# Key sums by fp32 adds on VectorE, one tile transposed by DMA, two denominators side by side: a linear-attention and MLP block on one core

## The chip, the core and the metric

The kernel runs on one core of one Trainium2 chip. The metric is the device time of one execution in microseconds, as the median of several runs. A core has TensorE (matmuls into PSUM, whose eight banks hold 128 x 512 fp32 each), VectorE, ScalarE and GpSimd, which work on SBUF and, GpSimd apart, on PSUM, and SyncE, whose queue here issues every DMA. Each engine takes its instructions in the order of its own queue. In the views of the profile PE is TensorE, PEld its weight loads, DVE VectorE, ACT ScalarE, POOL GpSimd and SP (SPq) SyncE.

## What is computed

```python
def phi(t): return where(t > 0, t + 1, exp(t)) + 1e-6

# A: linear attention, S = 2048 tokens, D = 512, 32 heads of 16
q, k, v = split(layernorm(x) @ wqkv)        # per head
pq, pk  = phi(q), phi(k)
kv  = einsum("bhsd,bhse->bhde", pk, v)
z   = einsum("bhsd->bhd", pk)               # sum of the keys over all tokens
num = einsum("bhqd,bhde->bhqe", pq, kv)
den = einsum("bhqd,bhd->bhq", pq, z)[..., None] + 1e-6
h   = x + merge_heads(num / den) @ wo
# B: MLP with 512 -> 1792 -> 512
out = h + relu(layernorm(h) @ w1) @ w2
```

Inputs and output are bf16.

## The kernel before

The 2048 tokens are 16 tiles of 128 tokens and 4 blocks (chunks, numbered 0 to 3) of 512 tokens. Everything stays in SBUF. There are no loops over tiles in the program: the string ORDER lists about 700 words, each the name of a small operation with its arguments, and they are issued in that order. The order in which the words stand is the order of each engine's queue. Semaphores between the engines follow from the data, and each PSUM bank is named by hand in the words.

The words that matter here, with their lines in the kernel before:

- `lx.t.n` (L219) loads n token tiles from tile t, `lk`, `lq`, `lv`, `lo`, `l1`, `l2` (L222) load parts of the key, query, value, output, first and second MLP weights. `lq.0.2` and `lq.2.2` are the two halves of the query weights along the contraction.
- `S.t`, `A.t` (L237, L238): layernorm statistics of tile t and their aggregate, on VectorE. `R` (L243, L244): 1/std on ScalarE. `N.t` (L251): the normalised tile. `s`, `a`, `r`, `n` are the same for the second layernorm (L239, L240, L243, L244, L258).
- A normalised tile is transposed into `lnT` either on TensorE, `T.t` (L270, four 128 x 128 transposes into PSUM, then a copy `E.t` on ScalarE, L280, or `V.t` on VectorE, L283), or by a DMA, `X.t` (L291). For the second layernorm: `t.t` with `e.t` or `v.t` (L270, L286, L289), or `x.t` (L292).
- `K.t` (L299): the keys of tile t, four matmuls of 128 x 512. `Q.c.j` (L307): a quarter j of the transposed queries of block c.
- phi of keys: `F` (L317, Exp) and `U` (L320, Relu) on ScalarE, `M` (L324, min with 1, plus 1e-6) and `D` (L327, add) on VectorE, for two tiles in one instruction in most places. `qF`, `qU`, `qM`, `qD` are the same for queries, L317 to L327.
- `G.t` (L351): four matmuls that add tile t's share to the product of the normalised tokens and the keys, in PSUM banks 4 to 7, over all 16 tiles. `gA`, `gD` (L373, L376) copy it out.
- `z.j` (L359): quarter j of the sum of the keys over the tokens, by 16 matmuls, one for each tile, each with a 128 x 128 weight load of keys and one column of ones. `zc`, `zh` (L365, L368) copy it and spread it over heads.
- `kv`, `kx`, `m` (L381, L389, L393), `mD` (L399): the small products that give, for each head, one matrix m that holds kv and wo.
- Denominators: `d4.c` (L406, four matmuls for block c), `dl4`, `dx4` (L412, L417: Ln, then Exp of minus that, on ScalarE, into `ld` and `rd`). For block 0 they are spread to rows by `rp` and `rm` on TensorE and VectorE (L422, L428), for blocks 1 to 3 they go through DRAM: `wb.c` (L434), eight `rb.c.h` (L437), and `dm` (L444) multiplies the queries by them.
- `h.t`, `hD.t` (L453, L459): the attention output and its addition to x.
- `p.c.f` and `ph` (L468, and L477 for half blocks): the MLP's up-projection; `pA`, `pD` (L483, L488): Relu on ScalarE or VectorE. `f.t` (L497): the down-projection of a tile, `fo` (L505) the scaled addition, `fd` (L512) the store.
- `warm` (L234): matmuls on zeros at the start.

The keys of tiles 0 and 1 lie in `pk_lo`, those of tiles 2 to 15 in a buffer that the MLP uses later (`acts[0]`). In the order before, tiles 0 to 5 are transposed on TensorE and 6 to 15 by DMA; for the second layernorm, tiles 0 to 3 on TensorE and the others by DMA.

Of the kernel before, what the change touches and what calls it, by code (L numbers as in the profile page):

```python
# [15 lines left out]


ORDER = """
table const masks warm.70.7.64 warm.3.7 lx.0.1 S.0 lx.3.1 lx.2.1 lx.1.1 S.3 S.2 A.0 A.3 A.2 R.0.1 S.1 R.2.2
N.0.2.2 A.1 N.0.0.2 N.2 R.1.1 N.3 N.1 lk.0.2 lx.4.2 lk.2.2 T.0.3.2.2 warm.1.7 T.0.0.0.2 T.2.2 E.0.2.2 T.3.3  # L20
T.1.1 V.2 E.0.0.2 E.1 K.0.0 lx.6.2 S.4 E.3 S.5 A.5 A.4 F.0.1 R.4.2 U.0.1 S.7 S.6 M.0.1 N.4 K.2.2 K.1.1 F.1.1
U.1.1 K.3.3 D.0.1 A.6 A.7 R.6.2 M.1.1 N.5 lx.8.4 D.1.1 N.7 T.4.0 G.0 T.5.1 F.2.1 E.4 E.5 U.2.1 S.9 S.8 N.6
M.2.1 A.9 A.8 D.2.1 F.3.1 R.8.2 U.3.1 G.1 K.4.0 K.5.1 F.4.2 U.4.2 M.3.1 S.10 N.8 D.3.1 A.10 S.11 M.4.2 N.9
D.4.2 A.11 lx.12.4 lq.2.2 X.7 X.6 lv.0.2 R.10.2 G.2 K.7.3 G.3 K.6.2 F.6.2 U.6.2 lq.0.2 X.8 X.9 S.13 S.12 A.13
N.11 N.10 A.12 M.6.2 X.11 X.10 D.6.2 R.12.2 G.4 G.5 K.8.0 K.9.1 F.8.2 U.8.2 N.13 S.14 N.12 S.15 A.14 A.15
M.8.2 D.8.2 R.14.2 N.15 N.14 G.6 G.7 K.11.3 K.10.2 X.13 X.12 lo.2.2 X.14 X.15 l1.2.2 l2.0.7 lo.0.2 l1.0.2
lv.2.2 l2.7.7 F.10.2 U.10.2 G.8 G.9 K.12.0 K.13.1 U.12.2 F.12.2 M.10.2 D.10.2 M.12.2 G.10 K.14.2 K.15.3
Q.0.0.0 Q.0.1.1 G.11 F.14.2 U.14.2 M.14.2 D.12.2 G.12 D.14.2 qF.0.0.2 qU.0.0.2 G.13 z.1.2 G.14 Q.0.3.1 z.0.2
Q.0.2.0 G.15 z.2.2 z.3.2 qU.0.2.2 qF.0.2.2 gD.0.2 zc gA.2.2 qM.0.0.2 Q.1.1.3 Q.1.0.2 qF.1.0.2 qU.1.0.2 kv.1.4
kv.0.4 kv.3.4 kv.2.4 zh qM.0.2.2 qD.0.0.2 qD.0.2.2 kx Q.1.2.0 m.0.4 m.1.5 d4.0.3 m.3.7 m.2.6 Q.1.3.1 dl4.0  # L30
dx4.0 Q.2.1.3 qF.1.2.2 qU.1.2.2 qM.1.0.2 mD.0.2 mD.2.2 rp.0.0.4 rp.0.3.7 rp.0.1.5 rp.0.2.6 Q.2.0.2 qM.1.2.2
rm.0.0.2 rm.0.2.2 qD.1.0.2 qD.1.2.2 Q.2.3.1 Q.2.2.0 qU.2.0.2 qF.2.0.2 h.0.4 h.1.5 Q.3.0.2 Q.3.1.3 hD.0 hD.1
s.0 s.1 a.0 h.2.6 a.1 n.0 n.1 hD.2 qF.2.2.2 qU.2.2.2 h.3.7 t.0.4 qU.3.0.2 qF.3.0.2 e.0 Q.3.2.0 d4.1.4 t.1.5
Q.3.3.1 hD.3 s.2 s.3 a.2 a.3 n.2 n.3 v.1 t.2.6 dl4.1 dx4.1 qF.3.2.2 qU.3.2.2 v.2 t.3.7 wb.1 ph.0.1.3.0
ph.0.0.2.0 rb.1.0 rb.1.4 rb.1.2 rb.1.6 rb.1.1 rb.1.7 rb.1.5 rb.1.3 v.3 ph.0.1.3.1 ph.0.0.2.1 pD.0.0.2 qM.2.2.2
ph.0.3.1.1 ph.0.2.0.0 ph.0.2.0.1 ph.0.3.1.0 p.0.4.2 p.0.5.3 pA.0.2.2 p.0.6.0 p.0.7.1 pA.0.6.2 pD.0.4.2 p.0.8.2
p.0.9.3 p.0.11.1 p.0.10.0 pA.0.8.2 dm.1.0.2 dm.1.2.2 h.6.6 hD.6 h.5.5 p.0.13.3 h.7.7 hD.5 qM.3.0.2 s.6 a.6 s.5
qM.2.0.2 n.6 a.5 qD.2.2.2 h.4.4 hD.4 f.2.6.0.7 p.0.12.2 s.4 qD.2.0.2 qD.3.0.2 qM.3.2.2 hD.7 a.4 n.5 s.7 a.7
pA.0.10.2 pA.0.12.2 r.0.4 n.7 n.4 f.0.4.0.7 f.0.4.7.7 f.2.6.7.7 f.3.7.0.7 fo.0 x.5 x.4 x.6 fd.0 d4.2.4 dl4.2
dx4.2 x.7 wb.2 f.1.5.0.7 f.3.7.7.7 f.1.5.7.7 p.1.1.1 p.1.0.0 p.1.2.2 p.1.3.3 rb.2.6 rb.2.0 rb.2.4 rb.2.2  # L40
rb.2.7 rb.2.5 rb.2.3 rb.2.1 fo.3 pA.1.0.2 fo.1 fo.2 pA.1.2.2 dm.2.2.2 dm.2.0.2 p.1.4.0 p.1.5.1 p.1.6.2 p.1.7.3
r.4.4 pA.1.4.2 p.1.8.0 p.1.9.1 h.11.7 h.10.6 h.8.4 pD.1.8.2 pA.1.6.2 p.1.10.2 p.1.13.1 p.1.11.3 pA.1.10.2 hD.8
s.8 hD.11 h.9.5 p.1.12.0 f.4.4.0.7 pA.1.12.2 hD.10 s.10 f.4.4.7.7 f.7.7.0.7 hD.9 s.11 a.11 s.9 a.9 n.11 n.9
a.8 a.10 n.10 qD.3.2.2 fo.4 n.8 x.11 x.9 x.8 x.10 d4.3.4 dl4.3 dx4.3 wb.3 fd.1 f.6.6.0.7 f.5.5.0.7 f.6.6.7.7
p.2.0.0 p.2.3.3 p.2.2.2 p.2.1.1 pA.2.0.2 pD.2.2.2 fd.3 rb.3.6 rb.3.0 rb.3.7 rb.3.4 rb.3.2 rb.3.1 rb.3.5 rb.3.3
fd.4 fd.2 f.5.5.7.7 p.2.4.0 f.7.7.7.7 fo.5 p.2.7.3 p.2.6.2 p.2.5.1 pA.2.4.2 dm.3.2.2 fo.7 dm.3.0.2 h.12.4
h.13.5 hD.12 fo.6 pA.2.6.2 p.2.9.1 p.2.10.2 p.2.8.0 pD.2.8.2 r.8.4 p.2.11.3 h.15.7 p.2.12.0 p.2.13.1 pA.2.12.2
pA.2.10.2 h.14.6 f.8.4.0.7 s.12 hD.15 hD.13 s.13 a.13 hD.14 f.10.6.0.7 a.12 n.13 n.12 s.14 a.14 s.15 a.15 n.15
n.14 fd.5 fd.6 x.12 x.15 f.11.7.0.7 f.8.4.7.7 f.9.5.0.7 f.10.6.7.7 fo.8 fd.7 x.14 x.13 f.11.7.7.7 f.9.5.7.7
p.3.1.1 p.3.0.0 pA.3.0.2 p.3.2.2 p.3.3.3 p.3.5.1 p.3.4.0 fo.9 pA.3.4.2 fo.11 pD.3.2.2 fo.10 p.3.7.3 p.3.6.2  # L50
p.3.9.1 p.3.8.0 pD.3.6.2 pD.3.8.2 f.14.6.0.7 f.13.5.0.7 p.3.13.1 p.3.10.2 p.3.12.0 p.3.11.3 pA.3.12.2 r.12.4
pD.3.10.2 f.12.4.0.7 f.14.6.7.7 f.13.5.7.7 f.12.4.7.7 fd.10 fd.8 fd.9 fd.11 fo.13 fo.14 fo.12 fd.12 fd.14
fd.13 f.15.7.0.14.0.2 fo.15.0.2 fd.15.0.2 f.15.5.0.14.3.1 fo.15.3.1 fd.15.3.1 f.15.4.0.14.2.1 fo.15.2.1
fd.15.2.1
"""


# [1 line left out]
def kernel(  # L59
# [149 lines left out]
    def op_masks():  # L209
        op_mask()  # L210
        op_maskh()


    def op_gate():
        nc.gpsimd.memset(wk_sb[:, 0:4:2, 0:1], 0.0)
# [4 lines left out]

    def load_d(dst, src, k, n, queue=None):
        (queue or nc.sync).dma_start(out=dst[:, k : k + n, :], in_=src[:, k : k + n, :])  # L222
# [126 lines left out]
    def op_G(t):  # L349
        for kd in range(KD):  # L350
# [2 lines left out]
                start=(t == 0), stop=(t == NT - 1),  # L353
            )

    def op_z(jb, b):
        at_bank["z"] = b
        for t in range(NT):
            nc.tensor.matmul(  # L359
                bk[:, b, jb : jb + 1], lhsT=pk(t)[:, 0, jb * P : (jb + 1) * P], rhs=ones[:],  # L360
                start=(t == 0), stop=(t == NT - 1),
            )
# [37 lines left out]

    def op_d4(c, b):
        at_bank["d4", c] = b
        for jb in range(KD):
            nc.tensor.matmul(  # L406
                bk[jb * Q4 : (jb + 1) * Q4, b, :], lhsT=zhd[:, jb, :], rhs=pqT[c][:, jb, :],
                start=True, stop=True,
            )
# [138 lines left out]
```

## Time and profile before

| | |
|---|---|
| time, median of 3 runs | 172.0 us (171.96 to 172.21) |
| profiled execution: its time, its span | 172.15 us, 170.4 us |
| TensorE busy | 165.1 us, 97% of the span |
| VectorE busy | 94.5 us, 55% |
| ScalarE busy | 66.3 us, 39% |
| granted TensorE clock | 1.0 in the mean |
| z matmuls (L359) | 64, in 1.54 us of the chain |
| transposes of the second layernorm on TensorE (L270, from hn) | 16, four tiles |

The span is what the profiler sees from the first to the last instruction; 1.75 us of the execution's time lie around it. A matmul is pipelined: the row of a 128 x 512 matmul gives 379 ns, but in a row of them the next starts 216 ns later, which is what a matmul more or less costs where TensorE is never idle. The same holds to a lesser degree for VectorE and ScalarE, whose next instruction starts some 0.1 us before the row of the last one ends; so durations from rows and times from start to start differ.

### The profile page before, as it was taken

Reading aid. Unit: us, or ns where it says so; the run is one execution under the profiler, and the core shown is the slowest. Engines: PE = TensorE matmul, PEld = TensorE weight load, DVE = VectorE, ACT = ScalarE, POOL = GpSimd, SP = SyncE. Lnnn points to the kernel's source line nnn. Section 1 sums busy time; section 2 is a strip of 40 time slices with the busy share of each in tenths; the row PEclk is TensorE's granted clock in tenths of the full one; section 3 lists DMA queues with packets and bytes.
Section 4 is the critical chain, followed back from the end, with each engine's and each line's share of the span. In section 5 each row is a group of like instructions: output and inputs, shape, how many; then the busy total and the mean of one; then the engine's idle time right before and its main releaser. Section 6 shows DMA issues by size and latency. Waiting matters only on the chain.

```text
span 170.4 us, 2460 instructions
## 1 busy us (share of the span) xinstructions
PE 165.1 (97%) x949; PEld 81.4 (48%) x966; DVE 94.5 (55%) x199; ACT 66.3 (39%) x98; POOL 4.7 (3%) x21
## 2 busy tenths in 40 slices
PE   7999999999999999999999999999999999999993
...
DVE  3999983215889945399050579105349613450252
...
GB/s 128 312 241 71 187 110 127 304 386 295 4 6 0 0 89 69 0 0 22 105 99 82 4 2 13 108 135 150 31 31 0 54 100 0 0 127 0 0 0 123
DMA packets 22619, 14.97 MB, mean 88 GB/s; under 512 B 13264, under 2 KB 21584, under 8 KB 22608
## 3 DMA queue, kind: packets, MB, share of 16 engines
...
q8 instruction: 7, 0.11, 0.3%
q14 instruction: 4, 0.03, 0.1%
...
## 4 chain that ended last, share of the span: by engine, by line
PE 87%; ACT 4%; DMA 3%; DVE 2%; SPq 2%; issue 1%
PE bk L497 28%; PE bk L468 26%; PE bk L307 8%; PE bk L453 8%; PE bk L299 5%; PE bk L351 5%; DMA wk_sb<-in_A_wqkv_dram 3%; PE bk L477 2%; ACT eb L317 2%; ACT rb L320 1%; SPq L219 1%; PE bk L359 1%; PE bk L406 1%; PE bk L393 1%; PE bk L270 1%
## 5 line engine op out<-in xcount | busy, mean ns | idle before, releaser
L497 PE MATMUL bk<-w_sb,at 128*128 128x512 bf16 (+2 forms) x247 | 49.8, 355 | 0.3
L468 PE MATMUL bk<-lnT,w_sb 128*128 128x512 bf16 x204 | 46.8, 379 | 0.2
L483 ACT ACTIVATE at<-bk 128x1024 bf16<-128x1024 f32 x19 | 19.2, 1023 | 65.7 <-PE bk L468 62.9
L497 PEld LDWEIGHTS <-at 128*128 128x128 bf16 x252 | 23.4, 98 | 25.2 <-issue 0.5
L468 PEld LDWEIGHTS <-w_sb 128*128 128x128 bf16 x208 | 20.4, 98 | 24.3
L488 DVE TENSOR_SCALAR at<-bk 128x1024 bf16<-128x1024 f32 x9 | 11.0, 1225 | 24.7 <-PE bk L468 23.3
L505 DVE SCALAR_TENSOR_TENSOR gT<-bk,rstd,h_nat 128x512 bf16<-128x512 f32 (+2 forms) x18 | 12.2, 689 | 20.0 <-PE bk L497 16.3
L320 ACT ACTIVATE rb<-bk 128x1024 bf16<-128x1024 f32 (+1 forms) x18 | 16.7, 927 | 7.1 <-PE bk L307 5.6
L317 ACT ACTIVATE eb<-bk 128x1024 bf16<-128x1024 f32 (+1 forms) x18 | 16.6, 928 | 4.2 <-PE bk L299 3.5
L299 PE MATMUL bk<-wk_sb,lnT 128*128 128x512 bf16 x63 | 15.2, 379 | 0.6 <-ACT rb L320 0.3
L307 PE MATMUL bk<-lnT,wq_sb 128*128 128x512 bf16 x62 | 15.2, 379 | 0.1
L453 PE MATMUL bk<-m_sb,pqs 128*128 128x512 bf16 x63 | 15.1, 379 | 0.0
L459 DVE TENSOR_TENSOR h_nat<-bk,x_nat 128x512 bf16<-128x512 f32 x16 | 10.8, 687 | 6.8 <-PE bk L453 6.6
L351 PE MATMUL bk<-at,h_nat 128*128 128x512 bf16 x54 | 13.4, 379 | 0.1
L237 DVE BATCH_NORM_STATS2 st<-x_nat 128x6 f32<-128x512 bf16 x16 | 10.3, 677 | 1.8 <-DMA x_nat<-in_A_x_dram 1.8
L239 DVE BATCH_NORM_STATS2 st<-h_nat 128x6 f32<-128x512 bf16 x16 | 10.7, 682 | 0.1
L324 DVE TENSOR_SCALAR eb<-eb 128x1024 bf16<-128x1024 bf16 (+1 forms) x18 | 7.0, 389 | 5.9 <-ACT eb L317 5.9
L299 PEld LDWEIGHTS <-lnT 128*128 128x128 bf16 x64 | 6.1, 98 | 8.2 <-DMA lnT<-h_nat 0.8
L453 PEld LDWEIGHTS <-pqs 128*128 128x128 bf16 x64 | 6.3, 98 | 7.5
L351 PEld LDWEIGHTS <-h_nat 128*128 128x128 bf16 x64 | 6.1, 98 | 6.8
L307 PEld LDWEIGHTS <-wq_sb 128*128 128x128 bf16 x64 | 5.9, 98 | 6.4 <-issue 0.2
L444 DVE TENSOR_TENSOR pqs<-pqT,rr 128x1024 bf16<-128x1024 bf16 x6 | 4.0, 688 | 5.5 <-DMA rr<-scr 5.2
...
## 6 DMA issues: line engine op xcount, KB each, us to landing
...
wk_sb<-in_A_wqkv_dram SPq DMA_DIRECT2D x2, 256.0 KB, 3.7
x_nat<-in_A_x_dram SPq DMA_DIRECT2D x2, 256.0 KB, 4.1
wq_sb<-in_A_wqkv_dram SPq DMA_DIRECT2D x2, 256.0 KB, 6.1
```

The lines of the kernel that those rows point to most:

```text
L299: nc.tensor.matmul(bk[:, b, :], lhsT=lnT[c][:, kd, j * P : (j + 1) * P], rhs=wk_sb[:, kd, :], start=(kd == 0), stop=(kd == KD - 1),)
L307: nc.tensor.matmul(bk[:, b, :], lhsT=wq_sb[:, kd, j * P : (j + 1) * P], rhs=lnT[c][:, kd, :], start=(kd == 0), stop=(kd == KD - 1),)
L317: nc.scalar.activation(out=buf(eb, kind, i, n), in_=bank(at_bank[kind, i], n), func=ACT.Exp)
L320: nc.scalar.activation(out=buf(rb, kind, i, n), in_=bank(at_bank[kind, i], n), func=ACT.Relu)
L351: nc.tensor.matmul(bk[:, KD + kd, :], lhsT=ln_nat[:, t, kd * P : (kd + 1) * P], rhs=pk(t)[:, 0, :], start=(t == 0), stop=(t == NT - 1),)
L453: nc.tensor.matmul(bk[:, b, :], lhsT=pqs[:, (c * KD + jb) % NQ, j * P : (j + 1) * P], rhs=m_sb[:, jb, :], start=(jb == 0), stop=(jb == KD ...
L459: nc.vector.tensor_tensor(out=h_nat[:, t : t + n, :], in0=bank(at_bank["h", t], n), in1=x_nat[:, t : t + n, :], op=ALU.add,)
L468: nc.tensor.matmul(bk[:, b, :], lhsT=w1_sb[:, kd, f * P : (f + 1) * P], rhs=lnT[c][:, kd, :], start=(kd == 0), stop=(kd == KD - 1),)
L483: nc.scalar.activation(out=acts[c % 2][:, f : f + n, :], in_=bank(at_bank["p", c, f], n), func=ACT.Relu)
L488: nc.vector.tensor_scalar(out=acts[c % 2][:, f : f + n, :], in0=bank(at_bank["p", c, f], n), scalar1=0.0, scalar2=None, op0=ALU.max,)
L497: nc.tensor.matmul(bk[:, b, 0 : w * P], lhsT=acts[c % 2][:, f, j * P : (j + 1) * P], rhs=w2_sb[:, f, k * P : (k + w) * P], start=(f == 0), ...
L505: nc.vector.scalar_tensor_tensor(out=o_t[:, t % NO, cols], in0=bk[:, at_bank["f", t, k], 0 : w * P], scalar=rstd2[:, t : t + 1], in1=h_nat ...
```

## The change

Three things, and a new ORDER in which they stand.

- Keys summed on VectorE: `za.t` adds the keys of two tiles at a time (128 x 1024) to an fp32 accumulator, five times for the 12 tiles 2 to 13; `zf` adds the accumulator's two halves, `zhi` rounds the sum to bf16 and `zlo` takes what the rounding left, again in bf16. `z.j` then needs six matmuls where it had 16: these two parts, and tiles 0, 1, 14 and 15.
- The first tile of the second layernorm is transposed by a DMA (`x.0` in place of `t.0` and `e.0`).
- `d4.2.0.2` computes the denominators of blocks 2 and 3 (the last two; they count from 0) one after the other, in two banks, where `d4.3` stood later; `ld` and `rd` get a part for every block.

```diff
+    ZT = 12
...
+    zacc = big.tile([P, 2, D], F32, name="zacc")
+    zhl = big.tile([P, 2, D], BF16, name="zhl")
...
-    ld = big.tile([P, 2, CW], F32, name="ld")
-    rd = big.tile([P, 2, CW], BF16, name="rd")
+    ld = big.tile([P, NCH, CW], F32, name="ld")
+    rd = big.tile([P, NCH, CW], BF16, name="rd")
...
+    def op_za(t):
+        nc.vector.tensor_tensor(out=zacc[:], in0=pk(2, 2) if t == 4 else zacc[:], in1=pk(t, 2), op=ALU.add)
+
+    def op_zf():
+        nc.vector.tensor_tensor(out=zacc[:, 0, :], in0=zacc[:, 0, :], in1=zacc[:, 1, :], op=ALU.add)
+
+    def op_zhi():
+        nc.vector.tensor_copy(out=zhl[:, 0, :], in_=zacc[:, 0, :])
+
+    def op_zlo():
+        nc.vector.tensor_tensor(out=zhl[:, 1, :], in0=zacc[:, 0, :], in1=zhl[:, 0, :], op=ALU.subtract)
+
     def op_z(jb, b):
         at_bank["z"] = b
-        for t in range(NT):
-            nc.tensor.matmul(
-                bk[:, b, jb : jb + 1], lhsT=pk(t)[:, 0, jb * P : (jb + 1) * P], rhs=ones[:],
-                start=(t == 0), stop=(t == NT - 1),
+        parts = [zhl[:, i, :] for i in range(2)] + [pk(t)[:, 0, :] for t in range(NT) if not 2 <= t < ZT + 2]
+        for i, part in enumerate(parts):
+            nc.tensor.matmul(
+                bk[:, b, jb : jb + 1], lhsT=part[:, jb * P : (jb + 1) * P], rhs=ones[:],
+                start=(i == 0), stop=(i == len(parts) - 1),
             )
...
-    def op_d4(c, b):
-        at_bank["d4", c] = b
-        for jb in range(KD):
...
+    def op_d4(c0, b0, n=1):
+        for c, b in zip(range(c0, c0 + n), range(b0, b0 + n)):
+            at_bank["d4", c] = b
+            for jb in range(KD):
...
```

The order is new from end to end. The places that matter, first before, then after:

```diff
-lx.0.1 S.0 lx.3.1 lx.2.1 lx.1.1 ... lk.0.2 lx.4.2 lk.2.2 T.0.3.2.2 warm.1.7 T.0.0.0.2 T.2.2 ... T.3.3 T.1.1 ... K.0.0 ... K.2.2 K.1.1 ... K.3.3
-lx.12.4 lq.2.2 X.7 X.6 lv.0.2 ... lq.0.2 X.8 X.9 ... X.11 X.10 ... X.13 X.12 lo.2.2 X.14 X.15 l1.2.2 l2.0.7 ...
-G.10 K.14.2 K.15.3 Q.0.0.0 Q.0.1.1 G.11 ... G.12 ... G.13 z.1.2 G.14 Q.0.3.1 z.0.2 Q.0.2.0 G.15 z.2.2 z.3.2 ... Q.1.1.3 Q.1.0.2 ... kv
-t.0.4 ... e.0 ... d4.1.4 t.1.5 ... wb.1 ph.0.1.3.0 ph.0.0.2.0 rb.1.0 ...
+lx.1.1 S.1 lx.0.1 S.0 lx.3.1 lx.2.1 lx.4.2 ... T.0.0.0.2 T.0.3.2.2 T.1.1 ... lk.0.2 lk.2.2 N.3 T.3.3 ... K.0.0 T.2.2 E.1 K.1.1 ... K.2.2 ... K.3.3
+lx.12.4 X.7 X.6 ... X.8 X.9 lq.0.2 ... X.13 X.12 ... za.4 X.10 X.11 lq.2.2 X.15 X.14 lv.0.2 l1.2.2 lv.2.2 l2.7.7 ...
+G.8 K.10.2 K.11.3 ... Q.0.0.0 Q.0.1.1 G.9 qU.0.0.2 M.12.2 za.6 M.10.2 D.12.2 D.10.2 za.8 za.10 K.14.2 K.15.3 G.10 ... G.13 ... Q.0.2.0 M.14.2 za.12 D.14.2 G.14 zf G.15 zhi zlo qM.0.0.2 qD.0.0.2 z.2.2 z.0.2 z.1.2 Q.0.3.1 z.3.2 zc gA.0.2 Q.1.1.3 Q.1.0.2 gD.2.2 ... kv
+d4.1.4 ... n.0 ... x.0 wb.1 rb.1.2 ... rb.1.1 l2.0.7 ... t.1.5 ... ph.0.3.1.0 ph.0.2.0.0 ...
```

After the word `G.4` the new order runs `K.8.0`, `K.9.1`, then `G.5`, `G.6`, `G.7`, `K.13.1`, `K.12.0` on TensorE.

More of the change, by code (lines that the diff above doesn't have):

```diff
@@ L18 @@
 ORDER = """
[L19 to L23, printed above, removed]
@@ L54 @@
-fd.15.2.1
+table const masks warm.70.7.64 warm.3.7 lx.1.1 S.1 lx.0.1 S.0 lx.3.1 lx.2.1 lx.4.2 A.1 S.3 A.0 R.1.1 R.0.1 S.2
+A.3 N.1 A.2 N.0.0.2 N.0.2.2 S.5 R.2.2 T.0.0.0.2 T.0.3.2.2 T.1.1 warm.1.7 E.0.2.2 E.0.0.2 lk.0.2 lk.2.2 N.3
+T.3.3 A.5 S.4 N.2 A.4 lx.6.2 K.0.0 T.2.2 E.1 K.1.1 R.4.2 V.3 F.0.1 U.0.1 F.1.1 U.1.1 V.2 K.2.2 N.4 T.4.0 F.2.1
+E.4 M.0.1 N.5 lx.8.4 D.0.1 S.6 S.7 M.1.1 A.6 A.7 D.1.1 S.8 R.6.2 G.0 T.5.1 K.3.3 K.4.0 E.5 G.1 K.5.1 U.2.1
+F.3.1 U.3.1 N.7 S.9 A.8 N.6 M.2.1 A.9 M.3.1 D.2.1 R.8.2 lx.12.4 X.7 X.6 F.4.2 U.4.2 G.2 D.3.1 N.8 S.13 N.9
@@ new lines @@
+A.13 M.4.2 S.12 D.4.2 A.12 R.12.2 G.3 K.7.3 K.6.2 X.8 X.9 lq.0.2 F.6.2 U.6.2 G.4 K.8.0 S.11 S.10 A.10 N.13
+A.11 M.6.2 N.12 K.9.1 R.10.2 U.8.2 F.8.2 D.6.2 X.13 X.12 S.15 N.10 A.15 S.14 A.14 N.11 M.8.2 D.8.2 R.14.2 N.15
+N.14 za.4 X.10 X.11 lq.2.2 X.15 X.14 lv.0.2 l1.2.2 lv.2.2 l2.7.7 lo.0.2 lo.2.2 l1.0.2 G.5 G.6 G.7 K.13.1
+K.12.0 G.8 K.10.2 K.11.3 F.12.2 U.12.2 F.10.2 U.10.2 Q.0.0.0 Q.0.1.1 G.9 qU.0.0.2 M.12.2 za.6 M.10.2 D.12.2
+D.10.2 za.8 za.10 K.14.2 K.15.3 G.10 G.11 G.12 G.13 F.14.2 U.14.2 qF.0.0.2 Q.0.2.0 M.14.2 za.12 D.14.2 G.14 zf
@@ new lines @@
+G.15 zhi zlo qM.0.0.2 qD.0.0.2 z.2.2 z.0.2 z.1.2 Q.0.3.1 z.3.2 zc gA.0.2 Q.1.1.3 Q.1.0.2 gD.2.2 qF.0.2.2
+qU.0.2.2 qF.1.0.2 qU.1.0.2 kv.2.4 kv.1.4 kv.3.4 kv.0.4 qM.0.2.2 zh qD.0.2.2 qM.1.0.2 kx qD.1.0.2 Q.1.3.1
+Q.1.2.0 qF.1.2.2 m.2.6 m.3.7 d4.0.3 m.0.4 m.1.5 mD.2.2 mD.0.2 Q.2.0.2 dl4.0 dx4.0 qU.1.2.2 Q.2.1.3 rp.0.3.7
+rp.0.0.4 rp.0.1.5 rp.0.2.6 Q.2.2.0 Q.2.3.1 qM.1.2.2 rm.0.0.2 rm.0.2.2 h.0.4 qD.1.2.2 hD.0 h.1.5 h.3.7 qU.2.0.2
+qU.2.2.2 qF.2.0.2 qF.2.2.2 d4.1.4 h.2.6 dl4.1 dx4.1 Q.3.2.0 Q.3.3.1 s.0 hD.1 a.0 hD.3 s.1 n.0 a.1 hD.2 n.1 s.3
@@ new lines @@
+s.2 a.3 qU.3.2.2 qF.3.2.2 x.0 wb.1 rb.1.2 rb.1.4 rb.1.6 rb.1.0 rb.1.7 rb.1.5 rb.1.3 rb.1.1 l2.0.7 a.2 n.3
+Q.3.1.3 t.1.5 Q.3.0.2 n.2 v.1 t.3.7 t.2.6 v.3 v.2 ph.0.3.1.0 ph.0.2.0.0 ph.0.3.1.1 ph.0.2.0.1 qF.3.0.2
+qU.3.0.2 pA.0.2.2 ph.0.0.2.1 ph.0.0.2.0 ph.0.1.3.1 ph.0.1.3.0 p.0.6.0 p.0.7.1 pD.0.6.2 dm.1.0.2 dm.1.2.2
+qM.2.2.2 qM.2.0.2 pA.0.0.2 p.0.5.3 p.0.4.2 p.0.11.1 p.0.10.0 h.6.6 qM.3.0.2 pA.0.4.2 hD.6 h.4.4 h.5.5 p.0.9.3
+h.7.7 p.0.8.2 pA.0.8.2 f.2.6.0.7 qD.3.0.2 qD.2.2.2 hD.5 qM.3.2.2 hD.4 s.6 qD.2.0.2 qD.3.2.2 a.6 n.6 hD.7 s.5
@@ new lines @@
+s.4 a.4 s.7 a.5 n.4 a.7 p.0.13.3 p.0.12.2 r.0.4 pD.0.12.2 pA.0.10.2 d4.2.0.2 dl4.3 dx4.3 f.0.4.0.7 dl4.2 dx4.2
+f.1.5.0.7 n.5 n.7 f.3.7.0.7 f.0.4.7.7 f.2.6.7.7 f.1.5.7.7 x.4 x.7 wb.2 x.5 x.6 p.1.1.1 p.1.0.0 rb.2.0 rb.2.4
+rb.2.6 rb.2.1 wb.3 rb.2.5 fo.0 rb.2.7 rb.2.2 rb.2.3 p.1.2.2 p.1.3.3 pD.1.0.2 p.1.5.1 p.1.4.0 pA.1.4.2 r.4.4
+pD.1.2.2 fo.2 dm.2.2.2 dm.2.0.2 f.3.7.7.7 p.1.8.0 p.1.6.2 h.10.6 hD.10 fo.1 fd.1 fo.3 rb.3.6 rb.3.2 rb.3.7
+p.1.7.3 h.8.4 pA.1.6.2 p.1.9.1 h.11.7 hD.8 f.4.4.0.7 p.1.10.2 hD.11 s.10 s.11 a.11 n.11 pA.1.8.2 p.1.13.1
```

68 lines of the change are left out of this document (21 added, 47 removed).

## The prediction

> **What bounds the kernel now.** I read the page's busy shares first, then the chain that ended last in order of time, then the timeline of the first 45 us engine by engine, then the transfers of a few narrow windows.
>
> ```profile
> span 170.4 us, 2460 instructions
> PE 165.1 (97%) x949; PEld 81.4 (48%) x966; DVE 94.5 (55%) x199; ACT 66.3 (39%) x98; POOL 4.7 (3%) x21
> PE   7999999999999999999999999999999999999993
> DVE  3999983215889945399050579105349613450252
> ```
>
> TensorE is full in every slice but the first and the last; VectorE is full only in slices 1 to 4 (4 to 21 us) and nearly idle in slices 6 to 8 (26 to 38 us).
>
> ```profile
> 8.28 2.33 PE bk L299 x10
> ...
> 20.81 1.90 PE bk L299 x8
> ...
> 36.52 0.38 PE bk L359 x16
> ...
> 38.65 0.38 PE bk L359 x16
> ...
> 40.78 0.78 PE bk L359 x32
> ...
> 56.41 0.22 PE bk L270 x4
> ```
>
> These are pieces of the chain that ended last: start, length, engine and line. From 8.28 us, when the second half of the key weights has landed, to 167.68 us the chain is TensorE but for one place. Adding up its queue from 8.28 at 216 ns per 128x512 matmul (8 take 1.73 us in the chain) lands on 20.39, and the next matmul starts at 20.81: one real gap of 0.42 us. So a matmul taken away is worth its own pace, unless another engine or a transfer then comes late.
>
> ```profile
> 18.66 1.89 PE L351 MATMUL bk<-at,h_nat 128*128 128x512 bf16 x8
> 20.80 1.41 PEld L299 LDWEIGHTS <-lnT 128*128 128x128 bf16 x8 [0.75 <-DMA lnT<-h_nat]
> 20.81 1.90 PE L299 MATMUL bk<-wk_sb,lnT 128*128 128x512 bf16 x8 [0.26 <-ACT rb L320]
> ```
>
> That is the gap in the timeline: K.8 waits for its transposed tile, issued at 16.55 behind two weight loads, and for a PSUM bank.
>
> **What the change removes on TensorE.** The key sums z take 16 matmuls in each of four columns; after, 6 (two parts of the fp32 sum, and tiles 0, 1, 14, 15). The chain gives 0.38 us for 16, 24 ns each: 40 fewer save 0.97 us. One tile's transposes (t.0, four at 55 ns, 0.22 us) go to a DMA: 0.22 us. Together -1.19 us, all on the path.
>
> **What it adds on VectorE.** Five fp32 adds of 128x1024, one of 128x512, a copy and a subtraction of 128x512. No row has an fp32 operand in SBUF. Bounds per wide add: 688 ns (bf16 add L327) and 1217 ns (L428, fp32 out of PSUM). I take the upper, which shares the 4-byte operand; start to start that is 1.14 us (two in 2.35 us). The Trainium skill, "VectorE: DVE Perf Modes", section "The perf-mode tier table", has fp32 tensor_tensor at one element a cycle, half the bf16 rate, with a formula that gives 1.22 us for 1024: the rule that speaks against this change, and it agrees with the end I took. For the rest I take 0.69, 0.42 and 0.69 us (rows of 128x512). In all 5 x 1.14 + 1.8 = 7.5 us, where VectorE stands idle (26 to 41 us).
>
> **Does it hide?** I laid the new order on the three engines with the start-to-start times of the timeline (stats 0.60, aggregate 0.09, normalise 0.32, min 0.34, add 0.61, Exp or Relu of two banks 0.92, matmul 0.216, results 0.17 us after the last start). The head, below, brings TensorE to 24.43 us with K.0 to K.9 and G.0 to G.7 done. Ten groups of four follow (K.13, K.12, G.8, K.10, K.11, Q.0.0, Q.0.1, G.9, K.14, K.15) at 0.864 us each: 33.07. Then F.14 ends 34.3, M.14 34.7, za.12 35.8, D.14 36.5; G.14, which waits for D.14, is due at 37.4 after G.10 to G.13 and Q.0.2: 0.9 us spare. The final add, copy and subtraction end at 38.2; the first z matmul is due at 39.1: 0.9 spare. The adds cost nothing as long as four G's and a Q cover them. Behind z.3 (40.56) come zc and then gT's second half (1.23 us), done 42.05; the kv matmuls, behind Q.1.1 and Q.1.0, are due at 42.3: 0.2 spare.
>
> **The head moves too.** Tile 1 is now first, so N.0 ends at 6.65 instead of 5.91; its two copies on ScalarE end at 8.05, and K.0 starts at 8.1 with all four matmuls ahead and T.2 behind it. Before, half of K.0 and T.2 were done by 8.28: 0.43 + 0.22 us more to do, from 0.18 us earlier. VectorE then runs almost without a break to 25 us, and D.2 (ends 15.75) holds G.2 for 0.13 us. Against that, K.8's transpose is issued at 16.5 with no weight load ahead and lands near 19.0, well before K.8 at 20.1: the 0.42 us gap goes. After K.0 to K.9 and G.0 to G.7 I reach 24.43 us; before it is 24.27. Head: +0.16 us, with ends -0.25 (no hold at G.2, chain 0.3 us shorter) and +0.6 (VectorE 3% slower over 17 us).
>
> **The query weights arrive late.** lq.2.2 was issued at 5.58; now it stands behind X.13, X.12, X.10 and X.11 on SyncE's queue.
>
> ```profile
> 19.87 1.19 SPq L291 DMA_TRANSPOSE lnT<-h_nat  x1
> 21.16 1.22 SPq L291 DMA_TRANSPOSE lnT<-h_nat  x1
> 25.05 0.57 SPq L222 DMA_DIRECT2D wo_sb<-in_A_wo_dram  x1
> wo_sb<-in_A_wo_dram SPq DMA_DIRECT2D x1, 256.0 KB, 3.0
> wq_sb<-in_A_wqkv_dram SPq DMA_DIRECT2D x2, 256.0 KB, 6.1
> ```
>
> The first three are starts on SyncE's queue: a transpose holds it 1.30 us. The others are transfers with the time to landing. X.13 starts when N.13 is done (20.73), so lq.2.2 goes at 20.73 + 4 x 1.30 = 25.93. Q.0.0's third matmul wants it at 24.43 + 5 x 0.864 + 2 x 0.216 = 29.18. A load of the same size behind a run of transposes (wo, 25.05) landed in 3.0 us: 28.93, 0.25 us before it is needed. The load of wv at 15.37 took 3.3, the wq half right behind it 4.3, the other wq half, in the opening rush, 7.9 (their median is the 6.1). I take 0.05 us of waiting; ends 0 and 1.05 (4.3 us). Behind that wait on TensorE stand Q.0.1, G.9, K.14 and everything after, and ScalarE's Relu of Q.0; nothing gives it back.
>
> **The middle.** x.0 waits for n.0 (54.6) and lands in 2.4 to 2.5 us, at 57.2; the up-projection ph of tiles 0, 1 is due at 58.1. Behind x.0 on SyncE's queue stand wb.1 (from 59.26 to 56.0, since d4.1 is earlier), eight rb and the late half of w2; the rb land near 64.2, dm.1 ends 66.1, h.6 is due at 66.9. The w2 half (896 KB; the first such load landed in 5.1) goes at 61.7 and is wanted at 72. The tight place is VectorE: from hD.0 to v.2 it runs 7.5 us unbroken, v.1 ends at 58.02 for ph at 58.04, and v.2 at 58.8 for 58.95. I add 0.1 us, ends 0 and 0.4. With d4.2 and d4.3 together, their inputs are ready 2 us before. For p.1, p.2 and p.3 the last transposes land 1.4, 1.0 and 2.3 us ahead, and by the same counting the three rr sets land before dm's turn on VectorE, whose results are in time by 0.8 us or more. In the tail the last two quarters of tile 15 still run last: 0.
>
> **Sum.** -0.97 - 0.22 + 0.16 + 0.05 + 0.1 = -0.88 us. The profiled execution took 172.15 us with a span of 170.4 and 1.75 around it; its span becomes 169.5. On the median of 172.0 the forecast is 171.1 us.
>
> **Rivals.** (1) A larger gain: no hold at G.2, no wait for wq, ph just in time: -1.19 - 0.25 = -1.44, 170.6. For it: wq lands at 28.9 by the nearest row. Chance 0.10. (2) The wait for wq, on the other side. Every microsecond of landing beyond 3.25 us is lost. With 4.3 us it costs 1.05 and the time is 172.1, no change: 0.09. From 4.6 us it is slower; with the 6.1 of its own median row the wait is 2.85 and the time 173.9. For it: 4.2 us transposes behind loads show how the transfers share; against: in the new order nothing but transposes is in flight with it. Chance 0.16. The Trainium skill, "TensorE: Matmul & The Clock Gate", section "Part 1: The HAM clock gate", halves the clock after an idle window of about 3.4 us, which would add up to an estimated 1.7 us to the worst case; no wait here is long enough to show it, the granted clock is 9 tenths or more in every slice. (3) VectorE's chain to z is the bound: fp32 adds of twice the price put za.12 1.14 us later, 0.25 past G.14; with the split also doubled, z waits about 0.9: 172.0. Against: nothing doubles the 1217 ns row. Chance 0.04. (4) x.0 takes 4.2 us like the transpose at 16.55: lands 58.9, ph waits 0.8: 171.9. Against: the transfers before it are long done. Chance 0.03.
>
> **How the numbers follow.** The forecast has 0.58, with a range of its own of 170.8 to 171.6. A measurement of this kernel can tell about 0.2%, 0.34 us. Faster: 0.58 + 0.10 = 0.68; within: 0.09 + 0.04 + 0.03 = 0.16; slower: 0.16. The range runs from 170.4 to 172.8, which takes in the level cases and the first part of (2), and leaves out some 0.05 below and 0.1 above.
>
> **What would show it.** Right: 24 matmuls on the z line, in about 0.44 and 0.15 us; TensorE's gap near 20.4 us gone; no idle before Q.0.0 near 29 us; the wide adds near 1.22 us; kv at 42.3 us against 43.1; TensorE's last matmul about 0.9 us earlier. Wrong: TensorE idle on wq_sb (rival 2), on D.14 or on the split sum (rival 3), or idle before the up-projection near 58 us.

## The result and the profile after

The changed kernel takes 170.75 us in the median of four runs (170.55 to 170.96), the kernel before 172.11 us beside it (171.96 to 172.24): a ratio of 0.9921, with a 95% interval of 0.9903 to 0.994. That is 1.36 us less, where 0.9 was forecast: the sign and the mechanism held, and 170.75 lies within the range. The profiled executions differ by less: 172.15 us with a span of 170.4 before, 170.96 with 169.2 after, so 1.19 us. The rest is where the executions fall within their spread. Of two experiments below (two more adds, the first time; tiles 0 and 1 in the sum) the profiled execution had every matmul slowed and took 446 and 983 us; it is used for nothing.

The page after, span, busy time and slices:

```profile
span 169.2 us, 2376 instructions
PE 163.5 (97%) x906; PEld 79.9 (47%) x922; DVE 101.0 (60%) x208; ACT 65.4 (39%) x96; POOL 4.7 (3%) x21
PE   7799999999999999999999999999999999999993
...
DVE  3989997896899908895127567326481200255323
```

TensorE is still full in every slice but the ends. VectorE has 6.5 us more to do, most of it in slices 6 to 8, which were nearly empty before. TensorE remains the bound.

The chain that ended last, after, in order of time (start, length, engine and line; L291 is K, L262 transposes, L343 G, L299 Q, L366 z, L388 kv, L461 h, L414 the denominators, L505 f):

```profile
3.61 4.93 DMA wk_sb<-in_A_wqkv_dram
8.58 0.59 PE bk L291 x2
...
20.20 1.86 PE bk L291 x8
...
39.33 0.43 PE bk L366 x18
39.76 0.89 PE bk L299 x4
40.64 0.13 PE bk L366 x6
...
42.52 0.89 PE bk L388 x16
...
49.68 1.23 DVE pqs L436
50.95 2.33 PE bk L461 x10
...
75.80 0.55 PE bk L414 x8
...
166.56 0.35 DVE gT L513
```

Four readings. The z matmuls are 24, in 0.43 + 0.13 us, against 1.54 before. K.8 follows the work ahead of it (20.20); of the gap of 0.42 us at 20.4 there remain 0.12 within the 1.86 us, K.9's wait for its tile from the transposing DMA, which landed at 20.98. TensorE's timeline lists no wait between 25 and 49 us. And at 49.68 the chain leaves TensorE for a VectorE multiplication: a wait in the first `h` that the prediction did not name.

How long the opening takes differs between executions of one kernel, as shown below. So the traces are also compared from the end of G.7, where the next K starts, to the last `fo`. TensorE's timeline before and after, and the chain's last piece before (`fo` is L505 there, L513 in the changed kernel):

```profile
24.27 1.89 PE L299 MATMUL bk<-wk_sb,lnT 128*128 128x512 bf16 x7
```

```profile
24.49 1.89 PE L291 MATMUL bk<-wk_sb,lnT 128*128 128x512 bf16 x7
```

```profile
167.68 0.35 DVE gT L505
```

That is 143.41 us before and 142.07 after (24.49 to 166.56): 1.34 less.

### The profile page after: what moved, and what is told of

Its sections match the earlier page's. It is cut to its first block, busy times and chain, and to the rows that moved or that the text cites. A ratio compares the mean times of both kernels' runs of the same rounds, so it can differ in the third digit from the quotient of the medians.

```text
span 169.2 us, 2376 instructions
## 1 busy us (share of the span) xinstructions
PE 163.5 (97%) x906; PEld 79.9 (47%) x922; DVE 101.0 (60%) x208; ACT 65.4 (39%) x96; POOL 4.7 (3%) x21
## 4 chain that ended last, share of the span: by engine, by line
PE 91%; DMA 3%; SPq 1%; issue 1%; DVE 1%
PE bk L505 29%; PE bk L476 26%; PE bk L343 8%; PE bk L461 8%; PE bk L291 8%; PE bk L299 7%; DMA wk_sb<-in_A_wqkv_dram 3%; PE bk L485 2%; SPq L212 1%; PE bk L262 1%; DVE pqs L436 1%; PE bk L414 1%; PE bk L400 1%; PE bk L388 1%; PE bk L366 0%
## 5 line engine op out<-in xcount | busy, mean ns | idle before, releaser
L505 PE MATMUL bk<-w_sb,at 128*128 128x512 bf16 (+2 forms) x248 | 50.7, 355 | 0.2
L476 PE MATMUL bk<-lnT,w_sb 128*128 128x512 bf16 x203 | 47.9, 379 | 0.2
L505 PEld LDWEIGHTS <-at 128*128 128x128 bf16 x252 | 23.5, 98 | 25.3 <-issue 0.4
L476 PEld LDWEIGHTS <-w_sb 128*128 128x128 bf16 x208 | 20.4, 98 | 24.3
L513 DVE SCALAR_TENSOR_TENSOR gT<-bk,rstd,h_nat 128x512 bf16<-128x512 f32 (+2 forms) x18 | 12.1, 689 | 21.6 <-PE bk L505 19.2
L461 PE MATMUL bk<-m_sb,pqs 128*128 128x512 bf16 x63 | 15.9, 379 | 0.3 <-DVE pqs L436 0.2
L291 PE MATMUL bk<-wk_sb,lnT 128*128 128x512 bf16 x62 | 15.3, 379 | 0.2 <-DMA wk_sb<-in_A_wqkv_dram 0.2
L299 PE MATMUL bk<-lnT,wq_sb 128*128 128x512 bf16 x62 | 15.2, 379 | 0.1
L343 PE MATMUL bk<-at,h_nat 128*128 128x512 bf16 x55 | 13.2, 379 | 0.1
L461 PEld LDWEIGHTS <-pqs 128*128 128x128 bf16 x64 | 6.1, 98 | 8.0 <-DVE pqs L436 0.7
L343 PEld LDWEIGHTS <-h_nat 128*128 128x128 bf16 x64 | 6.2, 98 | 7.3
L291 PEld LDWEIGHTS <-lnT 128*128 128x128 bf16 x64 | 6.1, 98 | 7.4 <-issue 0.5
L299 PEld LDWEIGHTS <-wq_sb 128*128 128x128 bf16 x64 | 5.9, 98 | 6.6 <-issue 0.2
L235 ACT ACTIVATE rstd<-mv,eps 128x2 f32<-128x2 f32 (+2 forms) x13 | 3.8, 295 | 7.0 <-DVE mv L230 4.7
```

The lines of the kernel that those rows point to most:

```text
L291: nc.tensor.matmul(bk[:, b, :], lhsT=lnT[c][:, kd, j * P : (j + 1) * P], rhs=wk_sb[:, kd, :], start=(kd == 0), stop=(kd == KD - 1),)
L299: nc.tensor.matmul(bk[:, b, :], lhsT=wq_sb[:, kd, j * P : (j + 1) * P], rhs=lnT[c][:, kd, :], start=(kd == 0), stop=(kd == KD - 1),)
L343: nc.tensor.matmul(bk[:, KD + kd, :], lhsT=ln_nat[:, t, kd * P : (kd + 1) * P], rhs=pk(t)[:, 0, :], start=(t == 0), stop=(t == NT - 1),)
L461: nc.tensor.matmul(bk[:, b, :], lhsT=pqs[:, (c * KD + jb) % NQ, j * P : (j + 1) * P], rhs=m_sb[:, jb, :], start=(jb == 0), stop=(jb == KD ...
L476: nc.tensor.matmul(bk[:, b, :], lhsT=w1_sb[:, kd, f * P : (f + 1) * P], rhs=lnT[c][:, kd, :], start=(kd == 0), stop=(kd == KD - 1),)
L505: nc.tensor.matmul(bk[:, b, 0 : w * P], lhsT=acts[c % 2][:, f, j * P : (j + 1) * P], rhs=w2_sb[:, f, k * P : (k + w) * P], start=(f == 0), ...
```

## The experiments

Each edit is shown as words of ORDER or as lines of the kernel, against the changed kernel (one against the kernel before). The differences are told beside the changed kernel's 170.65 to 170.75 us; each kernel ran beside the kernel before on its own chip, which took 172.17 to 172.25 us there, and the ratios are to that.

**The key sums on TensorE again.** The words `za.*`, `zf`, `zhi`, `zlo` go, and `z` is the loop of before:

```diff
-        parts = [zhl[:, i, :] for i in range(2)] + [pk(t)[:, 0, :] for t in range(NT) if not 2 <= t < ZT + 2]
-        for i, part in enumerate(parts):
+        for t in range(NT):
```

> The changed kernel with the key sums back on TensorE (16 matmuls a column, no fp32 adds), all else in the new order. Theory A, TensorE's queue is the bound and the adds are hidden: 40 matmuls at 24 ns come back, +0.97 us against the changed kernel, 171.7 us; the z line shows 64 matmuls in 1.55 us and the later pieces move by that. Theory B, the gain is the new order and the adds cost VectorE time that is felt: VectorE is 7.5 us freer, so at most +0.5 us, 171.2 or less.

Measured: 171.69 us (171.44 to 172.22), ratio 0.9972, interval 0.9952 to 0.9992: some 0.95 us over the changed kernel. The chain of this kernel (L352 is z, L298 Q):

```profile
39.05 1.18 PE bk L352 x48
...
41.12 0.38 PE bk L352 x16
```

64 matmuls take 1.56 us again at 24 ns each, on the path. From G.7's end to the last `fo` (24.21 to 167.29) it is 143.08 us, 1.01 more than in the changed kernel and 0.33 less than before, which is what the rest of the change is worth there. Theory A: the removed matmuls are worth their own pace, 0.97 us, and the adds cost nothing where they stand.

**The first tile's transposes on TensorE again.**

```diff
-Q.3.2.0 Q.3.3.1 s.0 hD.1 a.0 hD.3 s.1 n.0 ... x.0
+Q.3.2.0 s.0 hD.1 a.0 hD.3 s.1 n.0 t.0.4 e.0 Q.3.3.1
```

> The changed kernel with tile 0 of the second layernorm transposed on TensorE again (t.0 right behind Q.3.2, its copy on ScalarE), no DMA for it. Theory A: four transposes of 55 ns, +0.22 us, 170.97 us. Theory B: the copy on ScalarE comes late for the up-projection or Exp of Q.3 starts late and holds a bank: +0.5 us or more, with TensorE idle near 58.5 us.

Measured: 170.87 us (170.63 to 171.67), ratio 0.9936, 0.9911 to 0.9961. The medians are within each other's spread, so the traces decide. The chain of this kernel (L460 is h):

```profile
50.71 2.33 PE bk L460 x10
...
166.54 0.35 DVE gT L512
```

From where `h` goes on to the last `fo` it is 115.83 us, in the changed kernel 115.61 (50.95 to 166.56). The difference of 0.22 is the four transposes, A's number; TensorE waits nowhere for the DMA that replaces them.

**The denominators of blocks 2 and 3 apart.**

```diff
-d4.2.0.2 dl4.3 dx4.3 f.0.4.0.7 dl4.2 dx4.2
+d4.2.0 dl4.2 dx4.2 f.0.4.0.7 d4.3.1 dl4.3 dx4.3
```

> The changed kernel with the denominators of the last two blocks in two places, seven matmuls of the down-projection between them. The chain of the changed kernel has 0.55 us for the eight side by side and 0.33 for four alone. Theory A, the pairing itself saves on TensorE: +0.11 us, 170.86 us. Theory B, it only brings the work earlier: 0, and TensorE's last matmul at the same time.

Measured: 170.91 us (170.71 to 171.26), ratio 0.9933, 0.9911 to 0.9955; in its trace 50.50 to 166.33, 115.83 us, again 0.22 more than in the changed kernel. Neither theory had that size. The chain of this kernel (L413 is d4, L504 f):

```profile
75.35 0.33 PE bk L413 x4
75.68 1.62 PE bk L504 x7
77.29 0.33 PE bk L413 x4
77.62 5.07 PE bk L504 x23
```

and of the changed kernel at the same place:

```profile
75.80 0.55 PE bk L414 x8
76.34 6.58 PE bk L505 x30
```

Eight small matmuls in a row take 0.55 us, not twice 0.33: 0.11 saved. And the group of seven `f` after a `d4` takes 1.62 us where seven take 1.51 elsewhere in the changed kernel's chain (at 90.69): another 0.11. A group that stands alone costs about 0.2 more than one joined to another, and the change joins two. I had costed this part at nothing.

**The kernel before, with the adds alone.** Its order stays; `za.4` stands after `N.14`, `za.6 za.8 za.10` after `D.10.2`, `za.12 zf zhi zlo` after `D.14.2`, and `z.1` moves behind `G.14 Q.0.3.1`:

```diff
-G.13 z.1.2 G.14 Q.0.3.1 z.0.2
+G.13 G.14 Q.0.3.1 z.1.2 z.0.2
```

> The kernel before, in its old order, with only the key sums changed: the adds stand behind N.14, D.10 and D.14, and z's first column moves behind Q.0.3. Theory A: -0.97 us against before, 171.1 us, with 24 z matmuls in 0.59 us. Theory B, the old order has no room for the adds: the final sum (split done near 37.8 us) or D.12 comes late and TensorE waits, less than -0.5 us.

Measured: 171.28 us (170.88 to 171.82), ratio 0.995, 0.9934 to 0.9967: about 0.9 less than before; from G.7's end to the last `fo` (24.86 to 167.37) it is 142.51 us, 0.90 less. The first part alone carries two thirds of the change. Its chain still has the old order's gap:

```profile
17.10 4.25 DMA lnT<-h_nat
21.35 0.05 issue
21.39 1.90 PE bk L301 x8
```

K.8 waits for its transposed tile, which lands 4.25 us after its issue, behind the weight loads. So the gap goes by the new order, not by the adds.

**The changed kernel once more.**

> The changed kernel unaltered, to stand on the same chip as the three beside it and to show how its opening varies. In the runs so far the second half of the key weights landed between 8.2 and 8.8 us, in the old order too, and TensorE's last matmul moved with it. Theory A: 170.75 us as before within 0.2, and TensorE again waits about 0.36 us in h.0 near 50.6 us. Theory B, that wait was a chance of one execution: it is absent here.

Measured: 170.65 us (170.52 to 170.94), ratio 0.9911, 0.9886 to 0.9935. The wait in the first `h` is there again, of the same 0.36 us: no chance event. What changes between the two executions is the opening: here the second half of the key weights landed 4.1 us after its issue, not 4.9; K.0's four matmuls run unbroken, and the next K after G.7 starts at 24.05 instead of 24.49. TensorE's timeline:

```profile
7.77 1.03 PE L291 MATMUL bk<-wk_sb,lnT 128*128 128x512 bf16 x4
...
24.05 1.89 PE L291 MATMUL bk<-wk_sb,lnT 128*128 128x512 bf16 x8
```

The last `fo` stands at 166.12 instead of 166.56: from G.7's end on it is 142.07 us in both.

**Two more adds on VectorE.** Into a tile that nobody reads, so the output is unaffected:

```diff
+    def op_zx(t):
+        nc.vector.tensor_tensor(out=zdum[:], in0=zacc[:], in1=pk(t, 2), op=ALU.add)
...
-za.12 D.14.2
+za.12 zx.12 zx.12 D.14.2
```

> The changed kernel with two more fp32 adds of 128x1024 (into a tile that nobody reads) between za.12 and D.14. Theory A, the adds hide behind a slack of 0.9 us before G.14: 2.28 us more end D.14 1.4 us too late, G.14 waits 1.4 us, the time rises by 1.4 to 172.15 us. Theory B, VectorE is not near the path there: 0. Theory C, every add is paid in full: +2.3 us.

Measured: 172.53 us in the median of the eleven timed runs (172.18 to 173.03), ratio 1.0015, 1.0 to 1.003. The same kernel a second time:

> The kernel with two more fp32 adds between za.12 and D.14 again, since the recorded execution of the first was one with slow matmuls throughout and shows nothing. Its median rose by 1.9 us where 1.4 was expected. Theory A as before: G.14 waits 1.4 us and nothing else, so the 0.5 us above it is the spread of the opening. Theory B: a second wait stands behind it, on the split sum or on the copies of z and gT before kv, of about 0.5 us.

Measured: 172.52 us (172.21 to 172.87), ratio 1.0016, 1.0 to 1.0032. The timeline of VectorE and then of TensorE in this kernel (start, busy, engine, line, operation, in brackets the idle time before it and what ended it):

```profile
36.06 2.48 DVE L354 TENSOR_TENSOR zdum<-zacc,at 128x1024 f32<-128x1024 f32 x2
38.46 0.69 DVE L319 TENSOR_TENSOR at<-rb,eb 128x1024 bf16<-128x1024 bf16 x1
```

```profile
36.66 1.03 PE L299 MATMUL bk<-lnT,wq_sb 128*128 128x512 bf16 x4
39.20 1.89 PE L343 MATMUL bk<-at,h_nat 128*128 128x512 bf16 x8 [1.51 <-DVE at L319]
40.92 0.25 PE L369 MATMUL bk<-ones,zhl 128*128 128x1 bf16 x2
```

D.14 starts 2.6 us later than in the changed kernel (35.86 there), and G.14, at 39.20 instead of 37.44, waits 1.68 us from the end of Q.0.2's pace (37.52). So 2.6 us of delay cost about 1.7, and 0.9 were slack, which is A's number; its 1.4 us of waiting was short because the two adds delay D.14 by more than the 2.28 us it reckoned with. B's second wait, at z, does not come: z follows G with 0.04 us lost, since the split sum is done during the two G and ends, at 40.93, just as z starts. From G.7's end to the last `fo` (24.57 to 168.37) the trace has 143.80 us, 1.73 more than the changed kernel: the wait and no second one. By the medians the kernel loses 1.9 us; the other two tenths are not in this stretch of the trace, and nothing here places them.

**The last query weights behind two more transposes.**

```diff
-lq.2.2 X.15 X.14
+X.15 X.14 lq.2.2
```

> The changed kernel with the second half of the query weights loaded behind X.15 and X.14, 2.6 us later. Theory A: it goes at 28.4, lands 2.9 us later at 31.3, Q.0.0's third matmul, due at 29.24, waits 2.0 us and nothing gives it back: 172.8 us. Theory B, the wait lets K.14's transposes, VectorE and later loads run ahead and half of it is won back: 171.8 us. Theory C, the wait lowers the granted clock: more than 173.5 us.

Measured: 174.47 us (172.77 to 175.28, nine runs), ratio 1.0109, 1.0074 to 1.0144. TensorE's timeline in this kernel's profiled execution, which took 172.77 us (L298 is Q):

```profile
28.32 0.59 PE L298 MATMUL bk<-lnT,wq_sb 128*128 128x512 bf16 x2
31.05 1.47 PE L298 MATMUL bk<-lnT,wq_sb 128*128 128x512 bf16 x6 [2.14 <-DMA wq_sb<-in_A_wqkv_dram]
```

The load goes at 28.01 and lands 3.0 us later; Q.0.0's third matmul, due at 28.75, waits 2.30 us. That is the whole loss from G.7's end to the last `fo` (144.38 us, 2.31 more than the changed kernel). It explains 172.77 and not 174.47. Either the landing takes longer in the other executions, with other loads right behind it (A), or the wait has a second price (B). To tell them apart, the loads behind it were held back, by a store of `D.10`'s result on the same queue:

```diff
+    def op_hold(t):
+        nc.sync.dma_start(out=hold_d[:, :], in_=pk(t)[:, 0, :])
...
+X.15 X.14 lq.2.2 ... D.10.2 hold.10 lv.0.2 lv.2.2 l1.2.2 lo.0.2 lo.2.2 l2.7.7 l1.0.2 za.8 za.10
```

> As the kernel with the late query weights, but the loads that follow them (value, output and MLP weights) are held behind a small store that waits for D.10, so that nothing is in flight with the query weights but transposes. There the recorded execution waited 2.3 us and took 172.77, while most others took about 174.5. Theory A, the landing of the late half is lengthened in most executions by the loads issued within a microsecond behind it: alone it lands in 3 us always, 172.8 us with a narrow spread. Theory B, the clock or something else after the wait costs the other 1.7 us: the median stays near 174.5 us.

Measured: 174.58 us (172.97 to 175.13, six runs), ratio 1.0124, 1.0092 to 1.0155. With nothing behind the load the same two groups of times come, so A falls. The profiled execution, 172.97 us, has nearly the same wait, 2.24 us:

```profile
28.48 0.59 PE L299 MATMUL bk<-lnT,wq_sb 128*128 128x512 bf16 x2
31.15 1.47 PE L299 MATMUL bk<-lnT,wq_sb 128*128 128x512 bf16 x6 [2.08 <-DMA wq_sb<-in_A_wqkv_dram]
```

```profile
core 0: 171.3 us, clock 1.000
```

The line of core 0 is from the view of spans and mean granted clocks. Of the six executions, two have a mean clock of 1.0 and 0.999 and take 172.97 and 173.28 us; four have 0.989 or 0.99 and take 174.53 to 175.13. In the kernel before it the same: 172.77 to 173.68 at 0.999 to 1.0 (three), 174.46 to 175.28 at 0.988 to 0.99 (six). A mean lower by 0.01 over 173 us is 1.7 us lost, as much as 3.4 us at half clock would give, and 1.6 us is about what lies between the groups. Where in the span the clock falls, and to what, no trace shows, since both profiled executions are of the faster group. The wait of the slower group was not traced either; with the 1.7 us taken off, its times are those of the faster group, so it was probably as long. That the lower clock follows the wait is inferred from its absence in every kernel without so long a one, whose mean clock is 0.998 or more in each timed run (those with two more adds among them, which wait 1.68 us).

The Trainium skill, "TensorE: Matmul & The Clock Gate", section "Part 1: The HAM clock gate", has TensorE at half clock after an idle window of about 3.4 us. The size of the loss agrees. The window does not, if the lower clock is the wait's doing: the wait is 2.2 to 2.3 us in both traces, and 10 of 15 executions had the lower clock. Then the measurement decides.

**The first `h` in halves.** The changed kernel's only new wait, 0.36 us, is `h.0`'s third matmul waiting for the second multiplication `rm`. Here the first halves of `h.0` and `h.1` run first (`hh.t.b.half` is two of the four matmuls of `h.t`):

```diff
-h.0.4 qD.1.2.2 hD.0 h.1.5
+hh.0.4.0 hh.1.5.0 hh.0.4.1 qD.1.2.2 hD.0 hh.1.5.1
```

> The changed kernel with h.0 and h.1 each in two halves, issued h.0 first half, h.1 first half, h.0 second half, h.1 second half, so that 0.43 us of matmuls stand where TensorE waits 0.36 us for the second multiply by the denominators. Theory A: the wait in h.0 goes, but the copies v.1 to v.2 on VectorE, fed from hD.0 at 51.6, do not come earlier and hold the up-projection near 58.3 us: -0.2 us, 170.55 us. Theory B, the whole wait is won: -0.36 us. Theory C: the wait costs nothing, 0.

Measured: 170.63 us (170.42 to 170.95), ratio 0.9906, 0.9884 to 0.9928: nothing that can be told from the changed kernel's 170.65 on the same chip. TensorE's timeline in this kernel (L469 the halves of h.0 and h.1, L261 the transposes, L493 ph):

```profile
49.98 1.89 PE L469 MATMUL bk<-m_sb,pqs 128*128 128x512 bf16 x8
...
57.64 0.66 PE L261 MATMUL bk<-ident,hn 128*128 128x128 bf16 x8
58.28 1.91 PE L493 MATMUL bk<-lnT,w_sb 128*128 128x256 bf16 x16
```

The wait in `h` is gone, but TensorE now stands about 0.19 us before ph at 58.28 and some 0.09 before the transposes: VectorE is late next, there with a normalised tile (done at 57.60) and before ph with the copy v.1 of a transposed one (58.18). That is A's mechanism with less gain than its 0.2; from G.7's end to the last `fo` (24.30 to 166.30) 0.07 us remain. The prediction's tight place, VectorE before ph, is real, and the wait in `h.0` covers it.

**Tiles 0 and 1 in the sum too.** The accumulator takes 14 tiles, and z has four matmuls a quarter:

```diff
-in0=pk(2, 2) if t == 4 else zacc[:]
+in0=pk(0, 2) if t == 2 else zacc[:]
...
-if not 2 <= t < ZT + 2]
+if t >= ZT + 2]
...
-... za.4 ... za.6 M.10.2
+... za.2 ... za.4 za.6 M.10.2
```

> The changed kernel with tiles 0 and 1 also summed in fp32 (one more wide add, in VectorE's idle time near 29 us), so that each column of z takes 4 matmuls instead of 6. Theory A: 8 matmuls of 24 ns fewer, -0.19 us against the changed kernel, 170.5 us, and M.10 starts at most 0.1 us later. Theory B, VectorE's queue is full enough that D.10 or the split comes late: 0 or slower.

Measured: 170.31 to 170.90 us in the five timed runs, 170.37 in the middle; ratio 0.9898, 0.9878 to 0.9918. About 0.3 below the changed kernel, where 0.19 was expected; the two intervals overlap, so only the sign is likely.

**Both together.**

> The changed kernel with tiles 0 and 1 in the fp32 sum and h.0, h.1 in halves. Theory A: -0.19 us from z and -0.07 from the halves (the gap before the up-projection took most of the 0.36 us there), 170.4 us. Theory B, both end in the same later wait, on VectorE's copies v.2 and v.3 before the up-projection: less than -0.1 us.

Measured: 170.34 us (170.24 to 171.31), ratio 0.9896, 0.9874 to 0.9919, span 168.6. TensorE's timeline in this kernel (L365 is z):

```profile
38.81 0.19 PE L365 MATMUL bk<-ones,zhl 128*128 128x1 bf16 x2
...
39.11 1.02 PE L298 MATMUL bk<-lnT,wq_sb 128*128 128x512 bf16 x4
39.97 0.19 PE L365 MATMUL bk<-ones,zhl 128*128 128x1 bf16 x2
```

z takes 0.30 us for its first three quarters and 0.11 for the last, against 0.45 and 0.15 in the changed kernel's timeline, and TensorE waits for nothing there. From G.7's end to the last `fo` (24.13 to 165.93) it is 141.80 us, 0.27 less than in the changed kernel, A's 0.26 within a hundredth. By its median this is the fastest version run, 1.9 us under the kernel before, though its interval overlaps that of the changed kernel.

## Why the prediction was right, point by point

**The z matmuls: right, to 0.01.** -0.97 was forecast; 1.54 less 0.56 is 0.98 in the chain, and taking the part back (0.95) or doing it alone (0.9) gives the same.

**The adds hide: right, with its own margin.** VectorE's timeline after:

```profile
34.72 1.22 DVE L351 TENSOR_TENSOR zacc<-zacc,at 128x1024 f32<-128x1024 f32 x1
35.86 0.68 DVE L319 TENSOR_TENSOR at<-rb,eb 128x1024 bf16<-128x1024 bf16 x1
36.46 0.68 DVE L354 TENSOR_TENSOR zacc<-zacc 128x512 f32<-128x512 f32 x1
37.17 0.43 DVE L357 CAST zhl<-zacc 128x512 bf16<-128x512 f32 x1
37.64 0.69 DVE L360 TENSOR_TENSOR zhl<-zacc,zhl 128x512 bf16<-128x512 f32 x1
```

The wide add takes 1.22 us, the upper bound that was taken. D.14 ends at 36.54 and G.14 starts at 37.44: 0.9 us spare, as laid out. The split ends at 38.33 for z at 39.17: 0.84, laid out as 0.9. Two more adds then showed the price where the slack ends. Rival 3's mechanism is thus real, with the point from which it decides 0.9 us of delay; it was not reached. The kv matmuls stand at 42.36, forecast 42.3.

**t.0: right**, 0.22 by trace; x.0's landing makes nobody wait (rival 4 did not come).

**The head: mis-sized, and its number hit by luck.** +0.16 was forecast, 24.43 for G.7's end against 24.27. The changed kernel's two executions give 24.49 and 24.05. TensorE's timeline of the first:

```profile
7.57 0.40 PE L262 MATMUL bk<-ident,h_nat 128*128 128x128 bf16 x4 [0.20 <-DVE h_nat L243]
7.80 0.59 PE L291 MATMUL bk<-wk_sb,lnT 128*128 128x512 bf16 x2
8.58 0.59 PE L291 MATMUL bk<-wk_sb,lnT 128*128 128x512 bf16 x2 [0.18 <-DMA wk_sb<-in_A_wqkv_dram]
```

K.0 starts at 7.80, not at 8.1, and G.2 is not held; a landing 0.3 us later than before made up for both, so that 24.49 next to 24.43 is luck. What was taken as fixed was the landing of the second key weights: it took 4.6 us in the profiled execution of before (8.24), 4.9 in this one (8.54), and 3.6 to 5.1 across the kernels here. From that landing to G.7's end it is 16.03 us before and 15.95 after, and 16.08 with the adds alone in the old order (landing at 8.78). So at an equal landing this late the new order is about a tenth earlier, not 0.16 later. Where the landing comes at 8.2 us or earlier (seven traces), G.7 ends at 24.0 to 24.3, and K.0 starts at 7.7 to 7.9 as the transposes allow; what the old order does then no trace shows. The medians fit: -1.36 and, beside the changed kernel's second runs, -1.60, against -1.34 behind G.7's end, leave the head and the end of the kernel 0 to 0.3 us of gain. No experiment takes the head alone.

**wq: right on the place, 0.05 too dear.** Q.0.0 starts at 28.81 and no wait follows; the load landed in 3.1 us, at 28.9, within 0.05 of the forecast 28.93. Rival 2 did not come, but its price was shown by placing the load 2.2 us later: the wait itself and, in most executions, 1.7 us more at a lower mean clock, as much as the prediction's estimate from the Trainium skill had added.

**ph: wrong.** +0.1 was forecast, ends 0 and 0.4. ph starts at 58.54 without a wait, 0.91 earlier than before. The step that failed is the counting of VectorE's 7.5 us ahead of it: TensorE waits earlier, for `rm` in `h.0` (0.36 us), and this gives the copies their time. I said the middle's inputs were in time and missed this one, because only the transposes and the rows `rr` were followed, and not the multiplications ahead of the first `h`. The net is smaller than 0.36: before had a gap of 0.14 us ahead of ph itself (59.31, where eight transposes at their pace end, to 59.45) and a further tenth of small ones between 45 and 51 us, all gone. TensorE's timeline before:

```profile
58.86 0.66 PE L270 MATMUL bk<-ident,hn 128*128 128x128 bf16 x8
59.45 3.65 PE L477 MATMUL bk<-lnT,w_sb 128*128 128x256 bf16 x32
```

**The denominators: mis-sized.** 0 was forecast; they give 0.22.

**The sum.** From the profiled executions: -0.98 (z) - 0.22 (t.0) + 0.22 (head, with a landing 0.3 us later than in before) + 0.36 (`h.0`) - 0.25 (gaps of the middle) - 0.21 (denominators) = -1.08, against a measured -1.12 at the last `fo` (167.68 to 166.56). With an equal landing, the head's +0.22 is about -0.1, and the sum -1.40, near the -1.36 of the medians. So the forecast of -0.88 was 0.5 short, by the head (0.25) and the denominators (0.2) above all. That the middle's mistakes nearly cancel (+0.1 forecast, 0.36 - 0.25 measured) is luck. Rival 1, a larger gain of 1.44, was close in size. Of its three reasons no hold at G.2 and no wait for wq came true; ph in time did too, by way of another wait.
